# An attention and mixture-of-experts kernel on one core: the values products of the last 64 keys in quarters of the array, for both query groups at once

## The chip, the cores and the metric

The kernel runs on one core of a Trainium2 chip. TensorE does the matrix products (in the profile PE, its weight loads PEld), VectorE (DVE), ScalarE (ACT) and GpSimd (POOL) the work on rows, and SyncE (SP) issues every DMA. All data is fp32. The metric is the device time of one execution in microseconds; the changed kernel is compared with the kernel before on the same chip.

## The reference

Eight batches, eight heads, 576 positions, head size 64. First an attention with a bias from a small network on relative positions, then a soft mixture of experts over its output (512 wide, 32 slots, eight experts):

```python
scores = scale * np.matmul(q, k.transpose(0, 1, 3, 2))
...
bias = h @ w2
scores = scores + bias.transpose(2, 0, 1)[None, :, :, :]
scores = scores - np.max(scores, axis=-1, keepdims=True)
attn = np.exp(scores)
attn = attn / (np.sum(attn, axis=-1, keepdims=True) + 1e-09)
return np.matmul(attn, v).astype(np.float32)
```

The experts' part is `logits = x @ phi`, a softmax over all 4,608 tokens (dispatch) and one over the 32 slots (combine), `slot_input = d.T @ x`, two dense layers with a ReLU for each expert, and `c @ slot_out`.

## The kernel before, in words

A **unit** is one pair of heads of one batch: 4 pairs times 8 batches are 32 units, numbered pair by pair, so that units 24 to 31 are the last pair, where each batch's experts part is added. A unit's 576 queries are taken as row blocks p = 0 to 3 of 128 queries; the last 64 queries of two neighbouring units share a row block p = 4. The steps of a row block, named as in the order table:

- `S{p}.{n}`: the scores, half n of the keys, both heads at once: each product uses 64 rows of the array (line 438; line 443 for block 4, where four products use a quarter of the array each). Each head's result takes one of the eight PSUM banks.
- `t{p}.{head}{n}` (line 458, VectorE) adds the bias and finds the extreme, `e` (line 467, ScalarE) the exponential, `m` the reciprocal of the sums, `n` (line 373, GpSimd) the scaling.
- `T{p}` and `R{p}` (line 422) turn the weights so that keys lie on partitions: T the first 512 keys, R the last 64 of both heads, head 0 on partitions 0 to 63 and head 1 on 64 to 127. `c{p}` and `cR{p}` (line 376, ScalarE or VectorE) copy them to the tiles at0 (query group 0, blocks 0 and 1, 256 queries) and at1 (query group 1, the other 320 of each unit).

`M0` and `M1` (line 544) are the values products of the two query groups. Each is one accumulation in one bank over five blocks of keys, two heads each, every product on 128 rows and 64 columns of the array. For blocks 0 to 3 the 128 rows are 128 keys of one head. Block 4 holds the last 64 keys of *both* heads; its values come from the host in a form with zeros in the other head's 64 rows (`_apart`), so that half of the rows multiply zeros:

```python
for i in range(5):
    for hh in range(2):
        v0 = 64 * (4 * hh + i) if i < 4 else 512 + 64 * hh
        nc.tensor.matmul(po.t[64 * hh:64 * hh + 64, 0:w], d["v"][:, v0:v0 + 64],
                         main[:, :, 4 * hh + i, :] if i < 4 else x[:, r0:r0 + w], ...)
```

`x0` and `x1` copy the two results to a tile xts, and `xs` writes it to memory (line 557). `lq` and `lv` load a unit's queries and keys (line 342) and its values (line 347); `b0` to `b4` load the next pair's bias tiles bm and br (line 354), into five buffers for bm and one for br. `w` steps load expert weights (tile wt, lines 849 to 857), `fx` a batch's finished attention (tile xo, line 568). The experts' steps are `K`, `L` (line 611), `D` (lines 622 to 627), `W`, `Z` (lines 741 to 753), `C` and their copies; after the last one follow the two layers and the output (lines 961 to 1046).

Nothing here is scheduled at run time. The table `ORDER` lists every step as `name/unit`, in one sequence, with a + where a copy goes to VectorE instead of ScalarE; the steps are recorded in that order, so that it sets the order of the instructions on each engine and on SP's one queue. A PSUM bank is chosen at the step that first writes it, the one free the longest.

## Time and profile before

| | |
|---|---|
| time, median of 3 runs | 588.68 us (587.24 to 593.66) |
| the profiled execution | 590.42 us, span of the trace 588.6 us |
| TensorE busy | 557.2 us, 95% of the span |
| VectorE / ScalarE busy | 458.9 / 456.5 us, 78% each |
| GpSimd busy | 215.4 us, 37% |
| DMA | 111.90 MB, queue q1 53.9% of sixteen engines' time |

A busy TensorE is not yet a TensorE at its peak: an instruction counts as busy from its start to its modelled end, which overlaps its successor. What a group of products costs is read from the start of one group to the start of the next, or from the chain of waits, which lists them without overlap. An fp32 product shows as two records, so "x20" is ten products.

### The profile page before, as it was taken

The numbers are of one execution on the slowest core, as the hardware profiler recorded it, in microseconds if no ns is written. First come the engines' busy times: TensorE is split into PE (matmuls) and PEld (weight loads), VectorE is DVE, ScalarE is ACT, GpSimd is POOL, SyncE is SP. The second block draws the span as 40 slices with busy tenths as digits, with TensorE's granted clock in tenths as the row PEclk, the third lists the DMA queues.
The fourth block names the chain that finished last, engine by engine and source line by source line (L and its number), as shares of the span: only waits on it lengthen the run. The fifth ranks groups of instructions, "written<-read, shape, count | busy, mean of one in ns | idle before, by whom it ended". The sixth has DMA issues, their size and how long they took to land.

```text
span 588.6 us, 18890 instructions
## 1 busy us (share of the span) xinstructions
PE 557.2 (95%) x7175; PEld 356.9 (61%) x7175; DVE 458.9 (78%) x1807; ACT 456.5 (78%) x960; POOL 215.4 (37%) x311
## 2 busy tenths in 40 slices
PE   5899999999999999999999999799999999999993
PEld 3355666767666666666666666467666666653551
DVE  8999687888798887978898889487988988652323
ACT  6999789979978898887888798578767887841233
POOL 2001444554445446444445445244335223400000
PEclk9999899999999999999999999999999999999998
DMA  5599424044927364585515434821433406499988
GB/s 187 218 334 325 128 87 129 26 134 114 301 92 271 112 214 163 199 290 215 200 51 194 148 104 158 285 69 67 146 108 127 159 21 216 139 386 402 409 359 321
DMA packets 43322, 111.90 MB, mean 190 GB/s; under 512 B 7904, under 2 KB 8032, under 8 KB 43232
## 3 DMA queue, kind: packets, MB, share of 16 engines
q1 hardware_dynamic: 43232, 110.71, 53.9%
q8 instruction: 56, 0.92, 0.6%
q14 instruction: 34, 0.28, 0.1%
HBM read 83.28 MB, written 27.41 MB: 188 GB/s over the span
## 4 chain that ended last, share of the span: by engine, by line
PE 62%; DVE 12%; ACT 8%; DMA 7%; issue 5%; SPq 2%; POOL 2%; DVEq 0%; POOLq 0%; ACTq 0%
PE ps L544 17%; PE ps L438 15%; PE ps L422 12%; DVE y L458 6%; ACT y L467 3%; PE ps L443 3%; PE ps L1005 2%; PE ps L961 2%; DMA bm<-bias_m 2%; DMA xs<-xts 2%; PE ps L886 2%; POOL y L373 2%; SPq L354 2%; ACT e L896 2%; PE ps L611 2%
## 5 line engine op out<-in xcount | busy, mean ns | idle before, releaser
L373 POOL TENSOR_SCALAR y<-y,sm 128x576 f32<-128x576 f32 x288 | 210.5, 745 | 287.8 <-DVE sm L475 172.3
L467 ACT ACTIVATE y<-y,mn 128x576 f32<-128x576 f32 x288 | 221.1, 770 | 38.9 <-DVE mn L458 31.9
L544 PE MATMUL ps<-at,v 128*64 128x256 f32 (+1 forms) x1280 | 165.6, 409 | 1.3 <-DMA v<-in_v_dram 0.7
L376 ACT COPY at<-ps 128x1024 f32<-128x1024 f32 (+2 forms) x171 | 137.2, 817 | 27.7 <-PE ps L422 22.1
L438 PE MATMUL ps<-qk 64*128 64x288 f32 x1024 | 156.3, 422 | 1.9 <-DVE mn L458 1.7
L544 PEld LDWEIGHTS ps<-at,v 128*64 128x64 f32 x1280 | 88.5, 137 | 67.4 <-DVE mn L458 7.9
L458 DVE CUSTOM_DVE_ANT_0 y<-ps,bm,mn 128x288 f32<-128x288 f32 x256 | 123.1, 511 | 6.4 <-PE ps L438 2.9
L422 PEld LDWEIGHTS ps<-ident,y 64*128 64x128 f32 x2592 | 98.8, 140 | 43.3 <-issue 18.8
L458 DVE CUSTOM_DVE_ANT_0 y<-ps,bm 128x288 f32<-128x288 f32 x256 | 107.8, 453 | 21.6 <-PE ps L438 13.6
L422 PE MATMUL ps<-ident,y 64*128 64x64 f32 x2592 | 110.8, 228 | 6.7 <-POOL y L373 4.6
L438 PEld LDWEIGHTS ps<-qk 64*128 64x128 f32 x1024 | 95.2, 189 | 23.5 <-DVE mn L458 5.0
L467 ACT ACTIVATION_READ_ACCUMULATOR y<-y,mn 128x1 f32 x288 | 54.6, 190 | 0.0
L474 DVE TENSOR_SCALAR sm<-sm 128x2 f32<-128x2 f32 x144 | 38.0, 264 | 20.9 <-ACT y L467 20.4
L458 DVE DVE_READ_ACCUMULATOR2_ANT mn<- 128x1 f32 x576 | 47.5, 83 | 0.0
L886 PE MATMUL ps<-f,wbd 128*32 128x512 f32 (+49 forms) x640 | 42.0, 400 | 5.6 <-DVE f L877 3.3
L877 DVE TENSOR_SCALAR f<-tabs,scl,nb 128x560 f32<-128x560 f32 (+17 forms) x107 | 45.2, 496 | 1.4 <-PE ps L886 0.8
L376 DVE COPY at<-ps 128x256 f32<-128x256 f32 (+2 forms) x53 | 39.4, 743 | 8.3 <-PE ps L422 6.5
L886 PEld LDWEIGHTS ps<-f,wbd 128*32 128x32 f32 x640 | 20.8, 112 | 26.8 <-issue 9.3
L475 DVE RECIPROCAL sm<-sm 128x2 f32<-128x2 f32 x144 | 23.8, 166 | 4.9
L875 ACT ACTIVATE f<-tabs,cols,scl 128x416 f32<-128x416 f32 (+17 forms) x37 | 27.0, 791 | 0.0
L896 ACT ACTIVATE e<-ps,bcon 128x591 f32<-128x591 f32 x35 | 25.1, 784 | 0.0
L443 PE MATMUL ps<-qk 64*64 64x288 f32 x256 | 23.4, 435 | 0.0
(147 smaller groups left out, 361.6 us busy)
## 6 DMA issues: line engine op xcount, KB each, us to landing
wt<-in_moe_w_dram SPq DMA_DIRECT2D x62, 512.0 KB, 8.5
qk<-in_qk_dram SPq DMA_DIRECT2D x32, 608.0 KB, 4.1
v<-in_v_dram SPq DMA_DIRECT2D x32, 320.0 KB, 4.5
bias_m<-e SPq DMA_DIRECT2D x32, 295.5 KB, 3.6
out_dram<-ob SPq DMA_DIRECT2D x16, 512.0 KB, 5.2
xs<-xts SPq DMA_DIRECT2D x24, 288.0 KB, 4.5
xo<-xs SPq DMA_DIRECT2D x8, 864.0 KB, 5.0
bm<-bias_m SPq DMA_DIRECT2D x16, 288.0 KB, 3.9
```

Source lines behind the costliest of these rows:

```text
L373: nc.gpsimd.tensor_scalar(out=out, in0=y, scalar1=r, scalar2=1.0, op0=ALU.mult, op1=ALU.mult)
L376: (nc.vector.tensor_copy if eng else nc.scalar.copy)(out=out, in_=in_)
L422: nc.tensor.matmul(out, src[rs], ident[rs, rs], is_transpose=True, start=True, stop=True, tile_position=(64 * r, 0))
L438: nc.tensor.matmul(pss[hh].t[:, 0:HALF], x[rs, 640 + p * P:640 + (p + 1) * P], x[rs, k0:k0 + HALF], start=True, stop=True, tile_position=( ...
L443: nc.tensor.matmul(pss[hh].t[64 * r:64 * r + 64, 0:HALF], x[rs, 1152:1216], x[rs, k0:k0 + HALF], start=True, stop=True, tile_position=(64 ...
L458: nc.vector.tensor_tensor_reduce(out=d["y", p][:, hs], in0=d["ps", p, n][hh].read()[:, 0:HALF], in1=biases[hp][p][:, hs], scale=-QS, scala ...
L467: nc.scalar.activation(out=y, in_=y, func=AF.Exp, bias=d["mn", p][:, 2 + hh:3 + hh], scale=-1.0, accum_out=d["sm", p][:, hh:hh + 1])
L474: nc.vector.tensor_scalar(out=r, in0=r, scalar1=1e-9, scalar2=None, op0=ALU.add)
L544: nc.tensor.matmul(po.t[64 * hh:64 * hh + 64, 0:w], d["v"][:, v0:v0 + 64], main[:, :, 4 * hh + i, :] if i < 4 else x[:, r0:r0 + w], start= ...
L877: nc.vector.tensor_scalar(out=f, in0=tabs[:, 0:n], scalar1=sc, scalar2=nb1[:, 0:1], op0=ALU.mult, op1=ALU.max)
L886: nc.tensor.matmul(pb.t[32 * t:32 * t + 32, a // 512, a % 512:a % 512 + c1 - c0], wbd, x, start=True, stop=True, tile_position=(0, 32 * t))
L896: nc.scalar.activation(out=e, in_=x, func=AF.Identity, bias=bcon[:, k:k + 1])
```

## The change

Block 4 leaves `M0` and `M1`, which keep eight products each, and becomes a step `Mr`: four products that each use 64 rows and 64 columns of the array, one for each head and query group. For that query group 1 has its heads in exchanged halves of PSUM (and so of xts): head 0 of group 0 and head 1 of group 1 lie in partitions 0 to 63. Both groups' banks stay open from `M0` and `M1` until `Mr`. The values come without zeros (576 columns instead of 640), the keys of head 1 are rolled by 64 on the host instead of being stored twice (1,152 columns instead of 1,216). What R gives for group 0 goes to a tile of its own (`ar`, two buffers) instead of at0. Because of the exchange the experts' steps read some parts in other order, `phis` is kept a second time with its halves exchanged, and `rsum` shrinks to 32 columns, with its products split by columns. `ORDER` is a new table, with the step `Mr/u` added.

```diff
--- before.py
+++ after.py
@@ ORDER, two lines of some 176 @@
...
-S0.0/23 S0.1/23 e4.1/22 t2.11/22 t2.01/22 T1/22 m3/22 e4.0/22 e2.0/22 e2.1/22 n3.1/22 M1/21 n3.0/22 t0.10/23 t0.00/23
...
+T4/22 R4/22 t2.11/23 cR4/22 M0/22 K01/24 c4/22+ S3.1/23 t2.01/23 M1/22 t3.10/23 e1.1/23 t3.00/23 Mr/22 e0.0/23 m0/23
...
@@ -261,8 +262,8 @@
 
     ident = const.tile([P, P], F32, name="ident")
     make_identity(nc, ident)
-    rsum = const.tile([P, P], F32, name="rsum")
-    phis = const.tile([P, NP, NSL], F32, name="phis")
+    rsum = const.tile([P, 32], F32, name="rsum")
+    phis = const.tile([P, 2, NP, NSL], F32, name="phis")
     lp = xp.tile([P, 5 * P], F32, name="lp", tag="lp")
     et = xp.tile([P, 5 * P], F32, name="et", tag="et")
     et2 = xp.tile([P, 256], F32, name="et2", tag="et2")
@@ -294,13 +295,13 @@
 
     def ready():
 
-        nc.sync.dma_start(out=phis, in_=phi.rearrange("(g p) s -> p g s", p=P))
+        nc.sync.dma_start(out=phis[:, 0], in_=phi.rearrange("(g p) s -> p g s", p=P))
+        for r in range(2):
+            nc.sync.dma_start(out=phis[64 * r:64 * r + 64, 1], in_=phi.rearrange("(g r p) s -> p r g s", r=2, p=64)[:, 1 - r])
         nc.gpsimd.tensor_scalar(out=phis, in0=phis, scalar1=-1.0, scalar2=None, op0=ALU.mult)
-        nc.gpsimd.tensor_add(out=rsum[:, 0:32], in0=ident[:, 0:32], in1=ident[:, 32:64])
-        nc.gpsimd.tensor_add(out=rsum[:, 0:32], in0=rsum[:, 0:32], in1=ident[:, 64:96])
-        nc.gpsimd.tensor_add(out=rsum[:, 0:32], in0=rsum[:, 0:32], in1=ident[:, 96:128])
-        for r in range(1, 4):
-            nc.gpsimd.tensor_copy(out=rsum[:, 32 * r:32 * r + 32], in_=rsum[:, 0:32])
+        nc.gpsimd.tensor_add(out=rsum, in0=ident[:, 0:32], in1=ident[:, 32:64])
+        nc.gpsimd.tensor_add(out=rsum, in0=rsum, in1=ident[:, 64:96])
+        nc.gpsimd.tensor_add(out=rsum, in0=rsum, in1=ident[:, 96:128])
         for t in (lp, et, et2):
             nc.gpsimd.memset(t, 0.0)
 
@@ -338,12 +339,12 @@
 
 
         hp, b = units[u]
-        x = st[u]["qk"] = ldp.tile([P, 1216], F32, name="qk", tag="qk")
+        x = st[u]["qk"] = ldp.tile([P, 1152], F32, name="qk", tag="qk")
         nc.sync.dma_start(out=x, in_=qk[b, hp])
 
     def load_v(u):
         hp, b = units[u]
-        x = st[u]["v"] = ldp.tile([P, 640], F32, name="v", tag="v")
+        x = st[u]["v"] = ldp.tile([P, 576], F32, name="v", tag="v")
         nc.sync.dma_start(out=x, in_=v[b, hp])
 
     biases = [{} for _ in range(NP)]
@@ -432,15 +433,15 @@
             pss = d["ps", p, n] = [Banks(1), Banks(1)]
             for hh in range(2):
                 rs = slice(64 * hh, 64 * hh + 64)
-                k0 = 64 * (1 - hh) + n * HALF
+                k0 = n * HALF
                 if p < 4:
                     x = d["qk"]
-                    nc.tensor.matmul(pss[hh].t[:, 0:HALF], x[rs, 640 + p * P:640 + (p + 1) * P], x[rs, k0:k0 + HALF],
+                    nc.tensor.matmul(pss[hh].t[:, 0:HALF], x[rs, S + p * P:S + (p + 1) * P], x[rs, k0:k0 + HALF],
                                      start=True, stop=True, tile_position=(64 * hh, 0))
                 else:
                     for r in range(2):
                         x = st[u + r]["qk"]
-                        nc.tensor.matmul(pss[hh].t[64 * r:64 * r + 64, 0:HALF], x[rs, 1152:1216], x[rs, k0:k0 + HALF],
+                        nc.tensor.matmul(pss[hh].t[64 * r:64 * r + 64, 0:HALF], x[rs, S + 512:2 * S], x[rs, k0:k0 + HALF],
                                          start=True, stop=True, tile_position=(64 * hh, 64 * r))
 
         for n in range(2):
@@ -497,7 +498,7 @@
 
             o = st[u - u % 2] if c else d
             if ("at", c) not in o:
-                o["at", c] = atp.tile([P, (9, 54)[c] * (256, 64)[c]], F32, name="at", tag=f"at{c}")
+                o["at", c] = atp.tile([P, (8, 54)[c] * (256, 64)[c]], F32, name="at", tag=f"at{c}")
             return o["at", c]
 
         if p < 4:
@@ -516,8 +517,9 @@
                         half_turn(pt.t[:, r, 64 * i:64 * i + 64], d["y", q][:, 512:640], r)
 
             def keep_rest(eng):
-                o0 = (2048, 3136)[c]
-                o = target()[:, o0:o0 + 256].rearrange("a (i r n) -> a r i n", i=2, r=2)
+                if c == 0:
+                    d["ar"] = atp.tile([P, 256], F32, name="ar", tag="ar", bufs=2)
+                o = (target()[:, 3136:3392] if c else d["ar"]).rearrange("a (i r n) -> a r i n", i=2, r=2)
                 if p == 4:
                     o = target()[:, 3072:3456].rearrange("a (b i n) -> a b i n", i=1, n=64)[:, 0:6:5]
                 k = len(qs)
@@ -526,34 +528,47 @@
             step(u, f"R{p}", turn_rest)
             step(u, f"cR{p}", keep_rest)
 
-    def mix(u, c):
+    def mix(u):
 
         d = st[u]
         hp, b = units[u]
-        w = 256 + 64 * c
-
-        def products(_):
+        wide = (256, 320)
+
+        def source(c):
+            return (st[u - u % 2] if c else d)["at", c]
+
+        def products(c):
             po = d["po", c] = Banks(1)
-            x = (st[u - u % 2] if c else d)["at", c]
             b0 = u % 2 if c else 0
-            main = x[:, 0:(4, 6)[c] * 512].rearrange("a (b k n) -> a b k n", k=8, n=64)[:, b0:b0 + 4 + c]
-            r0 = (2048, 3072 + 64 * b0)[c]
-            for i in range(5):
+            main = source(c)[:, 0:(4, 6)[c] * 512].rearrange("a (b k n) -> a b k n", k=8, n=64)[:, b0:b0 + 4 + c]
+            for i in range(4):
                 for hh in range(2):
-                    v0 = 64 * (4 * hh + i) if i < 4 else 512 + 64 * hh
-                    nc.tensor.matmul(po.t[64 * hh:64 * hh + 64, 0:w], d["v"][:, v0:v0 + 64],
-                                     main[:, :, 4 * hh + i, :] if i < 4 else x[:, r0:r0 + w], start=i == 0, stop=i == 4,
-                                     tile_position=(0, 64 * hh))
-
-        step(u, f"M{c}", products)
-
-        def keep(eng):
+                    o = 64 * (hh ^ c)
+                    nc.tensor.matmul(po.t[o:o + 64, 0:wide[c]], d["v"][:, 64 * (4 * hh + i):64 * (4 * hh + i) + 64],
+                                     main[:, :, 4 * hh + i, :], start=i == 0, stop=False, tile_position=(0, o))
+
+        def rest(_):
+            r0 = 3072 + 64 * (u % 2)
+            keys = d["ar"], source(1)[:, r0:r0 + 320]
+            for hh in range(2):
+                rs = slice(64 * hh, 64 * hh + 64)
+                for c in range(2):
+                    o = 64 * (hh ^ c)
+                    nc.tensor.matmul(d["po", c].t[o:o + 64, 0:wide[c]], d["v"][rs, 512:576],
+                                     keys[c][rs], start=False, stop=True, tile_position=(64 * hh, o))
+
+        for c in range(2):
+            step(u, f"M{c}", lambda _, c=c: products(c))
+        step(u, "Mr", rest)
+
+        def keep(eng, c):
             if "xt" not in d:
                 d["xt"] = xp.tile([P, S], F32, name="xts", tag="xt", bufs=2)
-            cp(eng, d["xt"][:, 256 * c:256 * c + w], d["po", c].read()[:, 0:w])
-
-        step(u, f"x{c}", keep)
-        if c == 1 and hp < NP - 1:
+            cp(eng, d["xt"][:, 256 * c:256 * c + wide[c]], d["po", c].read()[:, 0:wide[c]])
+
+        for c in range(2):
+            step(u, f"x{c}", lambda eng, c=c: keep(eng, c))
+        if hp < NP - 1:
             step(u, "xs", lambda _: nc.sync.dma_start(out=xs[b, hp], in_=d["xt"]))
 
     def moe(u):
@@ -606,25 +621,29 @@
 
         def logits(_):
             pl = m["L"] = Banks(2)
-            for n in range(2):
+            for n, (a0, j0, j1) in enumerate(((256, 0, 256), (0, 256, S))):
                 for g in range(NP):
-                    nc.tensor.matmul(pl.t[32 * g:32 * g + 32, n, 0:HALF], phis[:, g, :],
-                                     X(g)[:, n * HALF:(n + 1) * HALF], start=True, stop=True, tile_position=(0, 32 * g))
+                    nc.tensor.matmul(pl.t[32 * g:32 * g + 32, n, a0:a0 + j1 - j0], phis[:, n, g, :], X(g)[:, j0:j1], start=True,
+                                     stop=True, tile_position=(0, 32 * g))
 
         step(u, "L", logits)
-        step(u, "lc", lambda eng: cp(eng, lp[:, 0:S].rearrange("a (x n) -> a x n", x=2), m["L"].read()[:, :, 0:HALF]))
+        step(u, "lc", lambda eng: cp(eng, lp[:, 0:S], m["L"].read().rearrange("a x n -> a (x n)")[:, 256:256 + S]))
         parts = ((0, slice(0, P)), (1, slice(P, 192)))
 
         def dispatch(_):
             pr = m["D"] = Banks(1 + fin, 3)
             if fin:
                 for n in range(2):
-                    nc.tensor.matmul(pr.t[:, n, 0:HALF], rsum, lp[:, n * HALF:(n + 1) * HALF], start=True, stop=True)
+                    for g in range(4):
+                        nc.tensor.matmul(pr.t[32 * g:32 * g + 32, n, 0:HALF], rsum, lp[:, n * HALF:(n + 1) * HALF], start=True,
+                                         stop=True, tile_position=(0, 32 * g))
                 return
             for cc in range(4):
-                nc.tensor.matmul(pr.t[32 * cc:32 * cc + 32, 0:P], rsum[:, 0:32], lp[:, cc * P:(cc + 1) * P], start=True,
+                nc.tensor.matmul(pr.t[32 * cc:32 * cc + 32, 0:P], rsum, lp[:, cc * P:(cc + 1) * P], start=True,
                                  stop=True, tile_position=(0, 32 * cc))
-            nc.tensor.matmul(pr.t[:, P:192], rsum, lp[:, 512:576], start=True, stop=True)
+            for g in range(4):
+                nc.tensor.matmul(pr.t[32 * g:32 * g + 32, P:192], rsum, lp[:, 512:576], start=True, stop=True,
+                                 tile_position=(0, 32 * g))
 
         step(u, "D", dispatch)
 
...
@@ -913,8 +938,7 @@
     for u, (hp, b) in enumerate(units):
         for p in range(5 - u % 2):
             rows(u, p)
-        for c in range(2):
-            mix(u, c)
+        mix(u)
         if hp == NP - 1:
             moe(u)
         if u >= 2:
@@ -932,7 +956,7 @@
     homes.update(wbr=(bsp, "br"), wat0=(atp, "at0"), wat1=(atp, "at1"), wv=(ldp, "v"), wxo=(xp, "xo"), wxt=(xp, "xt"),
                  wxk=(xp, "xk"))
     for k, home in homes.items():
-        step(U - 1, k + {"wv": " M1", "wxt": " K23 KR L x1"}.get(k, ""), lambda _, home=home: fetch_w(home, several.get(home[1], 1)))
+        step(U - 1, k + {"wv": " Mr", "wxt": " K23 KR L x1"}.get(k, ""), lambda _, home=home: fetch_w(home, several.get(home[1], 1)))
 
     csts, ends, hT2 = {}, {}, {}
 
...
-
 def _lay(q, k, v):
 
     B, H, S, D = q.shape
     q, k, v = (x.reshape(B, H // 2, 2, S, D) for x in (q, k, v))
     qt, kt = q.swapaxes(3, 4), k.swapaxes(3, 4)
-    kt = np.concatenate([kt[..., 512:], kt], axis=-1)
-    qk = np.concatenate([kt.reshape(B, H // 2, 128, 640), qt.reshape(B, H // 2, 128, 576)], axis=-1)
+    kt = np.stack([kt[:, :, 0], np.roll(kt[:, :, 1], 64, axis=-1)], axis=2)
+    qk = np.concatenate([kt, qt], axis=-1).reshape(B, H // 2, 128, 1152)
     vm = v[:, :, :, 0:512].reshape(B, H // 2, 2, 4, 128, D).transpose(0, 1, 4, 2, 3, 5).reshape(B, H // 2, 128, 512)
-    return qk, np.concatenate([vm, _apart(v[:, :, :, 512:])], axis=-1)
+    return qk, np.concatenate([vm, v[:, :, :, 512:].reshape(B, H // 2, 128, D)], axis=-1)
 
 
 def kernel(**inputs):
```

The table's lines tell nothing by themselves, so the order of the instructions is shown at three places. First TensorE around the values products of unit 12, before:

```order
L544 MATMUL ps<-at,v 64x320 x10
L544 MATMUL ps<-at,v 64x256 x10
L422 MATMUL ps<-ident,y 128x64 x20
L438 MATMUL ps<-qk 128x288 x4
L422 MATMUL ps<-ident,y 128x64 x16
```

and now:

```order
L547 MATMUL ps<-at,v 64x256 x8
L423 MATMUL ps<-ident,y 128x64 x18
L439 MATMUL ps<-qk 128x288 x4
L547 MATMUL ps<-at,v 64x320 x8
L557 MATMUL ps<-ar,v 64x256
L557 MATMUL ps<-at,v 64x320
L557 MATMUL ps<-ar,v 64x256
L557 MATMUL ps<-at,v 64x320
L423 MATMUL ps<-ident,y 128x64 x36
```

Twenty products in 128 rows and 64 columns have become sixteen and four quarters; here M0 comes ahead of M1, with transposes and scores between, so that M0's bank is held through them.

Second, TensorE around the scores of row block 4 of units 12 and 13 (line 443 before, 444 now), before:

```order
L438 MATMUL ps<-qk 128x288 x2
L544 MATMUL ps<-at,v 64x256 x10
L443 MATMUL ps<-qk 64x288 x8
L422 MATMUL ps<-ident,y 128x64 x20
L438 MATMUL ps<-qk 128x288 x8
```

and now:

```order
L423 MATMUL ps<-ident,y 128x64 x20
L444 MATMUL ps<-qk 64x288 x4
L557 MATMUL ps<-ar,v 64x256
L557 MATMUL ps<-at,v 64x320
L557 MATMUL ps<-ar,v 64x256
L557 MATMUL ps<-at,v 64x320
L444 MATMUL ps<-qk 64x288 x4
L423 MATMUL ps<-ident,y 128x64 x16
```

Here the quarter products of unit 11 stand between two groups of scores that divide the array in the same way.

Third, SP's queue where the last pair's bias tiles are loaded (units 22 to 24), before:

```order
L354 DMA br<-bias_r 64x512
L354 DMA bm<-bias_m 128x576
L354 DMA bm<-bias_m 128x64
L354 DMA bm<-bias_m 128x512
L557 DMA xs<-xts 128x576
L849 DMA wt<-in_moe_w_dram 128x1024
L568 DMA xo<-xs 128x3x576
L347 DMA v<-in_v_dram 128x640
L849 DMA wt<-in_moe_w_dram 128x1024
```

and now:

```order
L355 DMA bm<-bias_m 128x576
L355 DMA bm<-bias_m 128x64
L355 DMA bm<-bias_m 128x512
L348 DMA v<-in_v_dram 128x576
L572 DMA xs<-xts 128x576
L343 DMA qk<-in_qk_dram 128x1152
L348 DMA v<-in_v_dram 128x576
```

Each fence ends a few rows behind the last bias tile. Before, the results xs, a weight tile, the 864 KB of xo, values and another weight tile follow it; now xo stands ahead of br, no weights follow, and behind the last tile come a load of values, an xs and a load of queries and keys. The last three bm tiles now stand directly behind each other.

## Rows read from the trace of the kernel before

**Rows 1.** The page, part 1: busy time, share of the span, instructions.

```profile
PE 557.2 (95%) x7175; PEld 356.9 (61%) x7175; DVE 458.9 (78%) x1807; ACT 456.5 (78%) x960; POOL 215.4 (37%) x311
```

**Rows 2.** Windows by stage: length, busy time (instructions) by engine, clock, DMA share, GB/s.

```profile
16.00:60.00 44.00, 41.58 (x604) 21.07 (x596) 41.74 (x120) 42.88 (x72) 3.05 (x5) 1.00 0.81 290
...
440.00:480.00 40.00, 39.64 (x554) 25.22 (x550) 35.91 (x143) 32.21 (x76) 13.42 (x20) 1.00 0.33 112
480.00:520.00 40.00, 39.94 (x562) 25.45 (x562) 29.20 (x115) 30.84 (x75) 13.39 (x21) 1.00 0.52 177
520.00:588.60 68.60, 56.51 (x737) 29.33 (x729) 23.86 (x54) 20.94 (x42) 0.00 (x0) 0.96 0.95 376
```

**Rows 3.** Windows of two pairs of units in the middle, engines as above.

```profile
227.80:253.85 26.05, 25.83 (x324) 17.25 (x323) 22.48 (x96) 22.63 (x49) 13.18 (x18) 1.00 0.64 213
```

**Rows 4.** Chain of waits, 214.8 to 294.5 us: start, length, what, records.

```profile
273.30 2.84 PE ps L544 x20
...
281.37 5.00 PE ps L544 x40
...
292.18 2.31 PE ps L544 x20
```

**Rows 5.** TensorE's timeline: start, length, records, idle time before in brackets.

```profile
267.87 1.20 PE L443 MATMUL ps<-qk 64*64 64x288 f32 x16
269.00 0.34 PE L422 MATMUL ps<-ident,y 64*128 64x64 f32 x4
```

**Rows 6.** The same at 437 us, a single group of four.

```profile
437.05 0.72 PE L443 MATMUL ps<-qk 64*64 64x288 f32 x8
437.70 0.52 PE L422 MATMUL ps<-ident,y 64*128 64x64 f32 x9
```

**Rows 7.** The same at 294 us.

```profile
294.42 1.66 PE L443 MATMUL ps<-qk 64*64 64x288 f32 x16
296.02 0.65 PE L422 MATMUL ps<-ident,y 64*128 64x64 f32 x12
```

**Rows 8.** Groups of TensorE instructions by form: count, busy us, mean ns, idle before.

```profile
L443 PE MATMUL ps<-qk 64*64 64x288 f32 x256 | 23.4, 435 | 0.0
```

**Rows 9.** VectorE's timeline at 372 us.

```profile
372.50 0.08 DVE L458 DVE_READ_ACCUMULATOR2_ANT mn<- 128x1 f32 x1
377.04 0.46 DVE L458 CUSTOM_DVE_ANT_0 y<-ps,bm 128x288 f32<-128x288 f32 x1 [4.46 <-DMA bm<-bias_m]
```

**Rows 10.** SP's timeline there: when each DMA was issued.

```profile
369.59 1.48 SPq L354 DMA_DIRECT2D bm<-bias_m  x3
371.16 0.38 SPq L557 DMA_DIRECT2D xs<-xts  x1
371.58 0.43 SPq L849 DMA_DIRECT2D wt<-in_moe_w_dram  x1
372.06 0.43 SPq L568 DMA_DIRECT2D xo<-xs  x1
```

**Rows 11.** TensorE's timeline there.

```profile
378.04 0.71 PE L422 MATMUL ps<-ident,y 64*128 64x64 f32 x16 [1.02 <-DVE mn L458]
381.06 0.46 PE L422 MATMUL ps<-ident,y 64*128 64x64 f32 x8 [2.31 <-POOL y L373]
381.78 0.68 PE L422 MATMUL ps<-ident,y 64*128 64x64 f32 x12 [0.26 <-POOL y L373]
```

**Rows 12.** Windows of the stall and of what follows it.

```profile
376.00:382.00 6.00, 2.40 (x40) 1.56 (x38) 3.06 (x15) 3.20 (x8) 1.74 (x3) 1.00 0.96 344
382.00:386.00 4.00, 4.00 (x48) 2.48 (x46) 2.66 (x11) 1.60 (x3) 2.63 (x4) 0.57 0.56 164
```

**Rows 13.** The page, part 6: DMA issues, KB each, us to landing.

```profile
wt<-in_moe_w_dram SPq DMA_DIRECT2D x62, 512.0 KB, 8.5
...
bm<-bias_m SPq DMA_DIRECT2D x16, 288.0 KB, 3.9
```

**Rows 14.** TensorE's timeline at 567 us, four products in four strips of rows.

```profile
567.10 0.66 PE L1046 MATMUL ps<-sst,cR 32*64 32x256 f32 x8
567.69 1.07 PE L1005 MATMUL ps<-wt,hT 128*32 128x256 f32 x16
```

**Rows 15.** Timeline at 54 us: GpSimd's first use on y.

```profile
54.24 1.47 POOL L373 TENSOR_SCALAR y<-y,sm 128x576 f32<-128x576 f32 x2 [42.73 <-ACT e L896]
```

369 lines of the change are left out of this document (185 added, 184 removed).

## The prediction

> **What bounds the kernel now.** I read the busy shares first: TensorE 95%, VectorE and ScalarE 78% each [rows 1]. A mean hides stages, so the windows come next [rows 2]. From 16 to 60 us, where the bias tables are made, VectorE and ScalarE are full (41.74 and 42.88 of 44.00 us). In the middle, two neighbouring units take 26.05 us, of which TensorE is busy 25.83, VectorE 22.48 and ScalarE 22.63 [rows 3]. From 440 to 520 us TensorE is full again. In the tail from 520 us the DMA engines are busy 95% of the time. So between about 65 and 520 us a piece of TensorE's work that goes is worth its length, as long as nothing else fills the gap, and the other two engines have about 14% to spare.
>
> **What the removed products cost.** The chain of waits has the values products without overlap [rows 4]: ten of 320 columns 2.84 us, ten of 256 columns 2.31 us, and both behind each other 5.00 us. Apart they cost 0.15 us more than together, and the difference is one more change in how the array is divided. So one change costs 0.15 us, and five blocks of keys for both groups 5.00 - 0.15 = 4.85 us. One block of a unit is 0.97 us: 0.54 with 320 columns ((2.84 - 0.15)/5) and 0.43 with 256.
>
> **What the added products cost.** Products in quarters are in the trace: the scores of row block 4, 288 columns. Two groups of four take 1.13 us from their start to the next instruction [rows 5], one group 0.65 [rows 6]: one group more is 0.48, and 0.17 is the change of division. 288 columns in 0.48 us is the rate of 320 columns in 0.54, so four quarters run at once, and Mr takes 0.54 us, the longer of its two widths. Gain: 32 units x (0.97 - 0.54) = **13.8 us**. Against it stand the changes of division. Counted along TensorE's order, the array is divided in 232 stretches before and 249 now, because Mr stands alone in some places and beside products of its own kind in others: 17 x 0.15 = **2.6 us**. Net 11.2 us, the upper end.
>
> The trace shows no Mr, so the lower end needs a bound. Groups of four are not always that quick: two took 1.60 us at 294 us [rows 7], 0.47 more than the clean ones, and all 32 groups took 23.4 us [rows 8], 0.73 each, where a clean one with half a change is 0.57. If Mr pays the whole excess of 0.16 to 0.17, that is 32 x 0.165 = 5.3 us, and the gain is 5.9. Those scores are slow where a bank has not been read yet; Mr's banks are already held, but it must wait for two copies of the last keys. It is like them in part, so I take half of the excess, 2.6: a gain of **8.6 us**, with ends 5.9 and 11.2.
>
> **What the new order does to the stall at 377 us.** VectorE sat idle 4.46 us there for a bias tile of the last pair [rows 9]. It was issued at 369.59 us, and right behind it the queue got xs, 512 KB of weights and 864 KB of xo [rows 10]; it landed some 6 us later, where 3.9 is usual [rows 13]. TensorE stood still 1.02 + 2.31 + 0.26 us [rows 11]. After that idle time its granted clock fell: 0.57 in the mean from 382 to 386 us [rows 12], the lower level of 1.2 GHz for most of these 4 us, which loses another 0.43 x 4 = 1.7 us. The stall costs 5.3 us. In the new order neither weights nor xo follow these tiles, and between the issue of the second-last tile and its first use stand four adds of another block, some 2 us, and products. A landing in 3.9 us would still be waited for about 1 us. I take **4.3 us** as the gain, between 0 (the stall only moves to another tile) and 5.3.
>
> **The rest.** The three new small loads and the wider phis lie ahead of GpSimd's first use on y, before which it idles 42.73 us [rows 15]; without that cover they would be a few us once. Queries, keys and values shrink by 2.1 MB of 111.90 MB, which no wait in the middle asks for. The dispatch product over the last tokens is split by columns: its two changes of division go and are in the count of 17. Copies stay the same in number; some change between VectorE and ScalarE, and both have room [rows 3]. Four weight loads of 512 KB move from before unit 24 to after it; from 440 to 520 us the DMA share is 0.33 and 0.52 [rows 2], which hides them. Were the tail to wait for them, 2.1 MB at its 376 GB/s would be 5.6 us.
>
> **Sum.** The profiled execution took 590.42 us, of which the span is 588.6, and lies 1.7 above the median of the runs. 590.4 - 8.6 - 4.3 = 577.5; put on the median, 588.7 - 12.9 = **575.8 us**. Its own ends are 588.7 - 5.9 = 582.8 (slow Mr, stall moved) and 588.7 - 11.2 - 5.3 = 572.2.
>
> **Rivals.**
>
> *The new order saves more.* If it also sheds the excess of the scores in quarters, 5.3 us, by putting Mr and these scores beside each other: 588.7 - 11.2 - 5.3 - 5.3 = 567 us. For it speaks that about half of the 32 Mr stand so; against it, that these scores are slow for want of a read bank, which their place does not change.
>
> *The gain comes back as waits for banks.* M0's and M1's banks are held until Mr, with scores between that need two banks each. A score that finds its bank unread cost 0.47 us more [rows 5, 7]. One such wait in each unit is 15.0 us: 588.7 - 11.2 - 4.3 + 15.0 = 588.2, no change. For it speaks that VectorE, which reads the banks of the scores, is busy 86% of a pair of units [rows 3]; against it, that in about a quarter of the units M0, M1 and Mr stand directly behind each other.
>
> *The same wait twice a unit, and the kernel is slower.* Between M0 and Mr, TensorE's queue is in order: behind one waiting score stand the turns that feed the copies for Mr, and Mr behind those holds both banks longer. Two waits of 0.47 in each unit are 30.1 us: 588.7 - 15.5 + 30.1 = 603 us. It decides from (15.5 + 5.9)/32 = 0.67 us of new waiting in each unit. Against it: in the pair of units shown TensorE is idle only 0.22 us, so there is no sign of starved banks now.
>
> *The quarters do not run at once.* Mr's two halves of rows write the same two banks, in different partitions; the scores in quarters use a bank for each half of rows. The nearest row is the product of four strips of 32 rows in the output stage, where strips 0 and 1 write two halves of one bank: 0.59 us from its start to the next instruction [rows 14]. One strip behind the other in each bank would be at least 2 x 0.43 + 0.15 = 1.01. So the trace speaks against it. If Mr did run in two rounds, it would cost 1.08 us in place of 0.54: 32 x (0.97 - 1.08) = -3.5, less 2.6, so 588.7 + 6.1 - 4.3 = 590.5. The Trainium skill, "TensorEngine Tiling (Array Packing)", section "Restrictions and Gotchas", states this rival as a rule: different row tiles cannot access the same PSUM bank at the same time. By that rule Mr takes two rounds; the trace's row does not agree for disjoint partitions.
>
> **How the numbers follow.** A measurement of this kernel tells about 1% from no change. Forecast 56%, more saved 14%, gain eaten 15%, two rounds 5%, slower 10%. Predicted is the forecast's time, 576. The range takes in the saving order at its own low end (567 less 3 us, if still more waits go) and, above, the eaten gain, 588.2 with a little over: 564 to 589. Outside stay the two cases above it, 15%, and a few per cent below. Faster by over 1% means under 582.8: the forecast but for its upper edge (54%) and the saving order, 68%. Within 1%: that edge, the eaten gain and the two rounds, 22%. Slower by over 1%: 10%.
>
> **What the profile after would show.** Mr's four products take 0.54 us and a change of division, about 0.7 us from start to next start; 1.2 would mean two rounds. The values products of blocks 0 to 3 take 0.43 and 0.54 us a block as before. A pair of units in the middle takes 25.2 to 25.6 us instead of 26.05. VectorE's wait for bm near unit 24 is under 1.5 us, and TensorE's clock does not fall there. I am wrong if TensorE's waits on VectorE before scores or on copies before Mr pass 0.5 us a unit, or if the tail waits for weights.

## The result, and the profile after

The changed kernel took 583.78 us in the median of 13 runs (580.87 to 586.29), the kernel before 590.27 in as many on the same chip: 0.9891 of its time, 95% interval 0.9867 to 0.9915. It is faster by 1.1%; predicted were 2.2%. Two more sets of runs, each beside the kernel before on the same chip, gave 0.9876 [0.9836, 0.9916] and 0.9889 [0.9857, 0.9921]. Two of the 99 runs of the kernel before fell in a slower state of the chip and are left out of its means.

The page's first part answers to [rows 1]: TensorE works 10.9 us less, VectorE 6.3 less, ScalarE 3.5 more.

```profile
PE 546.3 (94%) x7235; PEld 351.7 (61%) x7235; DVE 452.6 (78%) x1808; ACT 460.0 (79%) x959; POOL 217.6 (38%) x308
```

Mr is line 557 now, the other values products 547, the scores in quarters 444. By form (count, busy us, mean ns, idle before), answering to [rows 8]:

```profile
L557 PE MATMUL ps<-at,v 64*64 64x320 f32 x128 | 23.9, 448 | 0.0
L444 PE MATMUL ps<-qk 64*64 64x288 f32 x256 | 22.6, 429 | 1.5 <-ACT at L377 1.2
L557 PE MATMUL ps<-ar,v 64*64 64x256 f32 x128 | 20.8, 395 | 0.0
```

One Mr in TensorE's timeline (start, length, records), with what stands ahead and behind:

```profile
243.96 0.34 PE L423 MATMUL ps<-ident,y 64*128 64x64 f32 x4 [0.20 <-POOL y L374]
244.23 0.43 PE L557 MATMUL ps<-ar,v 64*64 64x256 f32 x1
244.23 0.48 PE L557 MATMUL ps<-at,v 64*64 64x320 f32 x1
244.24 0.43 PE L557 MATMUL ps<-ar,v 64*64 64x256 f32 x1
244.25 0.48 PE L557 MATMUL ps<-at,v 64*64 64x320 f32 x1
...
244.55 0.44 PE L557 MATMUL ps<-at,v 64*64 64x320 f32 x2
244.71 1.26 PE L444 MATMUL ps<-qk 64*64 64x288 f32 x16
```

From its start to the next group's, which divides the array in the same way, are 0.48 us. All four products begin within 0.02 us, though two and two write halves of one bank, and together they take as long as one: the quarters run at once. Over all 32 units Mr takes 0.43 to 0.83 us from its start to the next instruction: 0.43 in the median where both neighbours have its own division, 0.70 where neither has.

Windows of pairs of units, as [rows 3], and the place of the old stall, as [rows 12]:

```profile
231.15:257.20 26.05, 25.64 (x325) 17.55 (x322) 22.10 (x96) 23.02 (x49) 12.54 (x18) 1.00 0.74 238
257.20:283.10 25.90, 24.89 (x314) 17.40 (x312) 20.11 (x91) 23.27 (x50) 12.87 (x18) 1.00 0.71 241
```

```profile
379.00:383.00 4.00, 4.00 (x62) 1.00 0.35 136
383.00:387.00 4.00, 4.00 (x35) 1.00 0.42 145
```

A pair takes hardly less than before, though TensorE has less to do in it. The stall is gone: full clock, TensorE never idle. In the whole trace VectorE's waits for tiles bm are down from one of 4.46 us [rows 9] to the row below (us in total, times, longest), and none of them lies near unit 24:

```profile
DVE y L459 <- DMA bm<-bias_m: 1.5, 2, 0.9
```

New are short waits of TensorE on the passage into the tail (timeline; idle time before in brackets), where the kernel before had two over 0.2 us, of 0.64 and 0.93:

```profile
509.22 0.42 PE L626 MATMUL ps<-xo,phis 128*32 128x256 f32 x3 [0.89 <-DMA xo<-xs]
...
514.30 0.49 PE L717 MATMUL ps<-ident,lp 32*128 32x32 f32 x5 [0.69 <-ACT lp L377]
...
517.01 1.43 PE L776 MATMUL ps<-xk,ek 128*32 128x128 f32 x40 [0.57 <-ACT ck L750]
518.92 0.33 PE L971 MATMUL ps<-ident,accs 128*128 128x128 f32 x1 [0.47 <-DVE accs L782]
519.60 1.92 PE L986 MATMUL ps<-wt,sT 128*32 128x512 f32 x16 [0.35 <-ACT sT L973]
```

The last row is the first product with experts' weights: the tail starts at 519.60 us, in the kernel before at 530.46. Up to there the trace shows a gain of 10.9 us (two more traces of the changed kernel, 10.0 and 8.8); end to end the runs show 6.5. So the question is what happens at and behind this place.

### The profile page after: what moved, and what is told of

Read it like the earlier page. It is cut to its first block, busy times and chain, and to the rows that moved or that the text cites. A ratio compares the mean times of both kernels' runs of the same rounds, so it can differ in the third digit from the quotient of the medians.

```text
span 579.5 us, 19040 instructions
## 1 busy us (share of the span) xinstructions
PE 546.3 (94%) x7235; PEld 351.7 (61%) x7235; DVE 452.6 (78%) x1808; ACT 460.0 (79%) x959; POOL 217.6 (38%) x308
## 4 chain that ended last, share of the span: by engine, by line
PE 64%; DVE 11%; ACT 10%; DMA 6%; issue 4%; POOL 2%; SPq 0%; ACTq 0%; POOLq 0%; DVEq 0%
PE ps L547 16%; PE ps L439 16%; PE ps L423 13%; DVE y L459 6%; ACT y L468 4%; PE ps L444 3%; PE ps L557 3%; PE ps L1030 2%; POOL y L374 2%; PE ps L986 2%; ACT f L900 2%; PE ps L911 2%; ACT e L921 2%; DMA bias_m<-e 1%; DMA xo<-xs 1%
## 5 line engine op out<-in xcount | busy, mean ns | idle before, releaser
L439 PE MATMUL ps<-qk 64*128 64x288 f32 x1024 | 160.2, 422 | 1.2 <-DMA qk<-in_qk_dram 0.4
L377 ACT COPY at<-ps 128x1024 f32<-128x1024 f32 (+2 forms) x151 | 132.1, 895 | 23.2 <-PE ps L423 19.3
L547 PE MATMUL ps<-at,v 128*64 128x320 f32 (+1 forms) x1024 | 133.7, 410 | 0.7 <-DMA v<-in_v_dram 0.4
L423 PE MATMUL ps<-ident,y 64*128 64x64 f32 x2592 | 113.3, 227 | 3.4 <-DVE mn L459 1.0
L439 PEld LDWEIGHTS ps<-qk 64*128 64x128 f32 x1024 | 100.3, 187 | 18.7 <-DVE mn L459 2.8
L547 PEld LDWEIGHTS ps<-at,v 128*64 128x64 f32 x1024 | 70.4, 137 | 54.6 <-DVE mn L459 6.9
L911 PE MATMUL ps<-f,wbd 128*32 128x79 f32 (+45 forms) x640 | 43.4, 407 | 7.0 <-DVE f L902 4.2
L911 PEld LDWEIGHTS ps<-f,wbd 128*32 128x32 f32 x640 | 22.8, 114 | 27.9 <-issue 10.1
L377 DVE COPY at<-ps 128x1024 f32<-128x1024 f32 (+2 forms) x41 | 31.2, 763 | 5.5 <-PE ps L423 5.0
L900 ACT ACTIVATE f<-tabs,cols,scl 128x432 f32<-128x432 f32 (+15 forms) x38 | 26.5, 753 | 2.5 <-DMA bias_m<-e 2.5
```

Source lines behind the costliest of these rows:

```text
L377: (nc.vector.tensor_copy if eng else nc.scalar.copy)(out=out, in_=in_)
L423: nc.tensor.matmul(out, src[rs], ident[rs, rs], is_transpose=True, start=True, stop=True, tile_position=(64 * r, 0))
L439: nc.tensor.matmul(pss[hh].t[:, 0:HALF], x[rs, S + p * P:S + (p + 1) * P], x[rs, k0:k0 + HALF], start=True, stop=True, tile_position=(64 * ...
L547: nc.tensor.matmul(po.t[o:o + 64, 0:wide[c]], d["v"][:, 64 * (4 * hh + i):64 * (4 * hh + i) + 64], main[:, :, 4 * hh + i, :], start=i == 0 ...
L900: nc.scalar.activation(out=f, in_=tabs[:, 0:n], func=AF.Relu, bias=cols[:, 1:2], scale=sc)
L911: nc.tensor.matmul(pb.t[32 * t:32 * t + 32, a // 512, a % 512:a % 512 + c1 - c0], wbd, x, start=True, stop=True, tile_position=(0, 32 * t))
```

## The experiments

All are edits of the changed kernel unless it says otherwise. The table has all runs of a kernel together, over several chips (the kernel before's from all sets of runs but the first); "lost" is one minus the mean granted clock, times the run's time. The kernel before's means differ by some 1.5 us from chip to chip, so where a difference is small it is also given against the kernel before on the same chip.

| kernel | runs | median us | mean us | clock | lost us |
|---|---|---|---|---|---|
| before | 84 | 589.66 | 589.86 | 0.9908 | 5.4 |
| changed | 25 | 583.46 | 583.55 | 0.9865 | 7.9 |
| last block in whole rows | 12 | 593.59 | 593.62 | 0.9861 | 8.3 |
| scaling halved | 5 | 578.21 | 578.63 | 0.9878 | 7.1 |
| scaling halved, whole rows | 12 | 589.84 | 590.00 | 0.9883 | 6.9 |
| waits filled | 18 | 581.48 | 581.41 | 0.9899 | 5.9 |
| before, waits filled | 12 | 591.02 | 590.56 | 0.9906 | 5.6 |

**The changed kernel again.**

> The changed kernel unchanged, for the others of this call to stand against. Every theory: 583 us or so (it took 583.78 in the median, 6.5 us under the kernel before), with its single runs spread from 581 to 586 us. Its trace shows whether a typical run loses its 2 us over the 581.3 us of the profiled one in one place (a stretch of lower granted clock, a late tile) or evenly; evenly if the granted clock alone does it.

582.74 us. Its trace has the clock low behind the first of the short waits (windows: length, TensorE busy, clock, DMA share, GB/s):

```profile
505.00:509.00 4.00, 3.15 (x28) 0.96 1.04 402
509.00:513.00 4.00, 4.00 (x48) 0.61 1.02 396
```

That is mostly the lower level of 1.2 GHz, behind a wait of 0.85 us. In the profiled execution both windows have 1.00, behind a wait of 0.89. A third trace of the changed kernel has the longest such wait, 1.75 us, and the clock stays full in it too. So it happens in some runs and not in others, not evenly, and the length of this one wait doesn't decide it.

**The products alone.**

```diff
-nc.tensor.matmul(po[c][o:o+64], v[rs, 512:576], keys[c][rs], tile_position=(64*hh, o))
+nc.tensor.matmul(po[c][o:o+64], v[:, 512:576], keys[c], tile_position=(0, o))
```

> The changed kernel's order and loads, but the last block of each unit again as two column pairs over whole rows (four products of 128 rows in two rounds instead of four quarters in one; the values are not separated by head there, so this part of the output is not the reference's). Theory A, the quarters save what they should on TensorE (0.43 us a unit) and the gain is lost elsewhere: 32 x 0.43 = 13.8 us slower than the changed kernel in the same call, 597 us, that is some 7 us slower than the kernel before, because the new order's 17 more changes of the array's division and its waits stay. Theory B, VectorE or ScalarE sets the pace in the steady middle and TensorE's saving is swallowed there: only 4 to 8 us slower than the changed kernel, 588 to 592 us. Theory C, the four quarters run in two rounds: no slower, 583 to 585 us.

593.59 us: 10.1 slower than the changed kernel by the means of all runs, 10.6 beside it on one chip. That lies between theories A and B; C is out. Against the kernel before it is 1.0052 [1.0025, 1.0079]: the same products in the new order, 3.2 us slower by the means on that chip, 3.8 against all runs. Its Mr:

```profile
248.55 0.65 PE L556 MATMUL ps<-ar,v 128*64 128x256 f32 x4
249.03 0.71 PE L556 MATMUL ps<-at,v 128*64 128x320 f32 x4
249.67 1.20 PE L444 MATMUL ps<-qk 64*64 64x288 f32 x16
```

1.12 us instead of 0.48, 0.15 of it a change of division. Added up over the 32 units, from start to next start, Mr takes 35.1 us here and 20.8 in the changed kernel: TensorE saves 14.2 us. This pair of runs splits the result: quarters -10.1, order +3.8 (on one chip -10.6 and +3.2). So some 4 us of what the quarters save on TensorE do not reach the end.

**Quarters in the old order.** Kernel before; in the 15 units where M1 and M0 already stand together, block 4 becomes quarters directly behind them.

```diff
-for i in range(5):            # blocks 0 to 4, each group
+for i in range(4 if u in QUARTERS else 5):
...
+# behind the second of M0, M1: four quarters for both groups
```

> The kernel before with its order and loads, and quarters only in the 15 units whose M0 and M1 already stand one directly behind the other (units 2 to 18 by twos, 23 to 29 by twos, 30 and 31). The exchange of the second group's heads is left out, so its part of the output is not the reference's. Its divisions change 245 times, 13 more than before. Theory A, TensorE's time is what counts and the new order gave gain back in waits: 15 x 0.43 less 13 x 0.15 = 4.5 us faster than the kernel before, 585.5 us, or 0.30 us a unit. Theory B, the copies and VectorE bound the middle: under 2 us faster, 588 to 590 us. If it gains more a unit than the changed kernel does (6.5 / 32 = 0.20 us), the new order costs something that this one does not.

597.93 us, 1.013 [1.0083, 1.0176] of the kernel before: neither theory. By the first scores of each unit its trace gained 0.6 us from unit 8 to unit 20; it lost 3.2 from unit 26 to unit 31 and 5.3 more up to the tail. In units 23, 25, 27, 29, 30 and 31 each xts is now complete only after both groups, and TensorE waits on the passage into the tail. That the one makes the other is my reading (timeline, windows):

```profile
512.19 1.96 PE L752 MATMUL ps<-xk,ek 128*32 128x256 f32 x16 [2.07 <-DVE ek L377]
```

```profile
508.00:512.00 4.00, 2.12 (x30) 0.99 0.00 1
512.00:516.00 4.00, 3.81 (x40) 0.58 0.00 0
534.00:538.00 4.00, 3.54 (x56) 0.73 0.93 331
538.00:542.00 4.00, 3.10 (x18) 0.50 1.01 346
```

Its tail starts at 539.34 us. The quarters hold both results to the end of the unit, and put into the old order they made the program slower.

**Weights earlier.** `w0/19` to `w0/23` moved to units 19 to 21.

> The changed kernel with the last five weight tiles (w0/19 to w0/23) loaded from unit 19 on, one a unit, instead of at units 27 to 29. Theory A, the 1.75 us that the end grew by, and the 0.9 us wait for an input of the tail, come from weight transfers that stand in the way of the tail's own loads and the outputs: 1 to 2.6 us faster than the changed kernel, 581 to 583 us. Theory B, the queue at the end is full with the outputs themselves: no change (within 0.5 us). Theory C, the weights now crowd the loads of units 19 to 23 and the stall at unit 24 is back: 2 to 5 us slower, 586 to 589 us.

582.79 us, no change: the weights are not it. In its trace the wait for the tail's input is 1.13 us and the outputs' last stretch 8.7 us, both as long as in the changed kernel's traces.

**Half of GpSimd's scaling.**

```diff
-nc.gpsimd.tensor_scalar(out=out, in0=y, scalar1=r, ...)
+nc.gpsimd.tensor_scalar(out=out[:, 0:288], in0=y[:, 0:288], scalar1=r, ...)
```

> The changed kernel, with GpSimd scaling only the first 288 of each score tile's 576 columns (the other half stays unscaled, so the output is not the reference's). This shortens one scaling from 0.75 us to about 0.4 us and brings each scaled tile some 0.35 us earlier to the transposes that wait for it; no other engine's work changes. In the steady middle a pair of units has two groups of 20 transposes that take 1.17 and 1.28 us instead of 0.65. Theory A, the softmax chain that ends at GpSimd keeps the rest of the quarters' gain in the middle: up to 0.35 us at two places a pair, some 15 pairs: 5 to 10 us faster than the changed kernel's 582.7 us, 573 to 578 us. Theory B, the throughput of VectorE or ScalarE (83% and 88% busy in the middle) keeps it: under 2 us faster, 581 to 583 us.

> The same half scaling together with the last block in whole rows (four products of 128 rows, two rounds, values not separated by head) instead of quarters; the output is not the reference's for both reasons. Against the run with half scaling and quarters this prices the quarters with the chain out of the way. Theory A (the chain swallowed what TensorE saved): the difference is larger than the 10.9 us measured with full scaling, 13 to 15 us (32 x 0.43 = 13.8 and four changes of division more, 0.6): 587 to 592 us, the same as or faster than the kernel before. Theory B (VectorE and ScalarE): the difference stays near 10.9 us, 592 to 594 us.

578.21 and 589.84 us: 4.9 and 3.6 faster by the means than with full scaling (one scaling took 0.51 us, not 0.4). The quarters are worth 11.4 us here against 10.1 to 10.6, nearer to theory B; the difference is no larger than its noise (standard error 0.8). So the full scaling keeps at most a small part of the quarters' gain. How much of the 4.9 and 3.6 is the chain through GpSimd is not shown: in both traces the last stretch behind the last copy, where GpSimd does nothing, is 7.75 us, against 9.3 and 9.0 with full scaling.

**The tail's input first.** `wy1 wbm2 wy2 fx/31` becomes `fx/31 wy1 wbm2 wy2`.

> The changed kernel, with the last input tile of the tail's first part (fx/31) issued ahead of the three weight loads that now stand directly before it on SyncE. Theory A, the changed kernel loses time at the passage into the tail, where TensorE waits 0.85 to 0.9 us for that tile 8.1 us after its issue (before it landed 5.1 us after) and the granted clock fell to half for some 3.5 us behind the wait in one of two traces: the wait goes, 0.9 us, and where the clock fell another 1.7 us, so 0.9 to 2.6 us faster than the changed kernel's median of 582.7 us, 580 to 582 us, with mean granted clocks of 0.989 to 0.992 more often than 0.982 to 0.986. Theory B, the clock falls elsewhere too (the other waits of 0.35 to 0.7 us at 515 to 520 us): 0.5 to 1 us faster, the clocks as before. Theory C, the three weights now come late to the tail: no change or slower.

583.06 us, no change, so theory A is out and B's 0.5 us do not show either. The 0.9 us wait is gone, but in this trace the clock fell at the next waits instead (0.70, 0.59, 0.47, 0.35 us at 512 to 519 us):

```profile
509.00:513.00 4.00, 3.30 (x65) 1.00 1.03 410
513.00:517.00 4.00, 3.41 (x73) 0.72 1.02 393
517.00:521.00 4.00, 3.17 (x24) 0.50 1.05 405
```

This fall has a price that can be read. From the tail's first product to the end of the last copy the changed kernel takes 50.6 us, and so does every trace in which the clock is full from the tail's start on; here, with the low clock reaching some 2.7 us into the tail, it takes 52.0.

**The stall alone, in the kernel before.** `fx/24` ahead of `lq/24`, `w0/21` and `w0/22` to units 18 and 19.

> The kernel before, products and order of TensorE untouched; only its loads are moved so that the bias tile that VectorE waits 4.46 us for near 375 us comes earlier: the input tile fx/24 is issued ahead of lq/24, and the weights w0/21 and w0/22 three and five units earlier. Theory A, as the prediction had it: the stall's 3.6 us of idle TensorE and the fall of the clock behind it, 5.3 us in all, are saved, 585 us. Theory B, most of what is saved there comes back as waits further on, as it seems to have done in the changed kernel: 588 to 590 us. Theory C, another load is late in its place: no change, 590 us or more.

590.88 us, 1.0017 [0.9993, 1.0042]. The edit took only part of the stall (timeline of VectorE; windows of TensorE):

```profile
377.05 0.46 DVE L458 CUSTOM_DVE_ANT_0 y<-ps,bm 128x288 f32<-128x288 f32 x1 [2.50 <-DMA bm<-bias_m]
```

```profile
376.00:382.00 6.00, 4.29 (x58) 1.00 0.41 149
382.00:386.00 4.00, 4.00 (x48) 0.57 0.55 149
```

The clock still fell. From unit 22's first scores to unit 26's this trace takes 57.7 us, the kernel before 59.6; so 1.9 us were saved there, and the runs are no faster. New waits came elsewhere, one of 1.7 us for an xs on VectorE and one of 1.0 on TensorE behind it. With part of the stall left it does not test the stall's whole price.

**The old opening.** The first 378 steps in the kernel before's order, the rest in the new one.

> The changed kernel with the opening in the order of the kernel before: all steps up to the first scores of unit 2 stand as they stood there (with unit 0's quarters put behind its M1), everything behind them as in the changed kernel. Theory A, the new order gives back in the opening what it saves later: the scores of unit 2 began at 79.0 us in the changed kernel and at 77.4 us before, although one unit's quarters (0.4 us) were already saved there, and unit 2 of the run with whole rows began at 79.9 us. Then this kernel is 1.6 to 2.5 us faster than the changed one's 583.4 us (median of 31 runs of it and of two versions that took the same time), 581 to 582 us. Theory B, the opening's loss is made up further on by waits that are there anyway: no change, within 0.7 us.

593.45 us: it tests neither theory. The seam has stalls of its own; the scores of unit 2 began at 86.9 us instead of 79.0. The opening's 1.6 us stay a reading of single traces, which scatter: unit 2 begins at 77.4 to 78.5 us in four traces with the old order's opening and at 78.5 to 80.4 in eight with the new one's. Together with filled waits:

> The old opening and the filled waits together. If each is worth what its theory A says, 1.6 to 2.5 us and about 2 us, they add: 579 to 580 us, 1.8% under the kernel before. If the opening's gain is swallowed, 581 to 582 us; if neither holds, 583 us.

593.18 us, the same seam.

**Filled waits.** Transposes of the identity into the bank that the waiting product writes next, 3, 2, 2, 1 and 1 of them:

```diff
+def fill(bank, n):
+    for _ in range(n):
+        nc.tensor.transpose(out=bank[:, 0:P], in_=ident, identity=ident)
```

> The changed kernel with nine transposes of the identity (0.27 to 0.33 us each) put into five waits of TensorE on the passage into the tail (0.85, 0.70, 0.59, 0.47 and 0.35 us in the traces), each group less than its wait, so that it is busy in them; their results are overwritten. Theory A, the changed kernel's typical runs lose about 2 us to a granted clock that falls to half behind these waits (the traces show it at 508 to 513 us in one run and at 514 to 521 us in another; its runs lost 7.8 us of full clock in the mean, those of the kernel before 5.7): the falls are gone, the mean granted clock is 0.990 or more, 581 to 582 us. Theory B, the clock falls there for another reason, or elsewhere: no change, 583 to 584 us, clocks of 0.982 to 0.989 as before. Theory C, the fillers themselves come late: 0.3 to 1 us slower.

> The changed kernel with nine transposes of the identity in five waits on the passage into the tail, once more. Its first six runs had granted clocks of 0.990 or more in five, but stood to the kernel before on that chip as the changed kernel did on others (0.9891). Theory A, the falls of the clock there cost about 2 us: beside the changed kernel on the same chip it is 1 to 2 us faster, with a mean clock of 0.989 or more. Theory B, the time they cost is lost anyway (the tail's transfers or the outputs set the end): the clock is higher, the time the same within 0.5 us. Theory C, the six clocks were chance: clock and time as the changed kernel's.

> The filled version of the changed kernel a third time, beside it: 0.985 to 0.989 of the kernel before, 581.5 us in the middle, clock 0.990. Its trace shows a third time whether the stretch from the last copy to the end is 7.5 us, as in its first two traces, or 8.4 to 9.3, as in the three of the changed kernel.

581.82, 580.79 and 581.15 us; 0.9891 [0.9850, 0.9932], 0.9849 [0.9816, 0.9882] and 0.9856 [0.9825, 0.9887] of the kernel before. The changed kernel beside the second took 583.22 us. All runs together: 2.1 us faster than the changed kernel (standard error 0.4); with each measured against the kernel before on its own chip, 1.4 us (standard error 0.7). A mean clock under 0.988 came in 15 of 25 runs of the changed kernel and in 1 of 18 of this one. The first six runs left it open (the clock up, the ratio as before); the three sets together speak for theory A, with a gain of 1.4 to 2.1 us.

**The same in the kernel before**, five transposes in its two waits:

> The kernel before, with five transposes of the identity in its own two longer waits on the passage into the tail (0.64 and 0.93 us in its trace). Theory A, the falls of the clock there belong to the changed kernel's passage with its five waits: the kernel before gains nothing from it, within 0.7 us of 590 us, its mean granted clock stays at about 0.990. Theory B, the falls are as frequent in both: 1 to 2 us faster, 588 to 589 us, and the 2 us that the filled version of the changed kernel gained say nothing of this change.

591.01 us, 1.0014 [0.9989, 1.0038]; clock 0.9906, without them 0.9908. By this interval there is no more than 0.7 us to gain there: the loss on the passage belongs to the changed kernel.

**The opening filled too**, eight more transposes at 60 to 65 us:

> Also eight transposes in three waits of unit 0 (1.04, 0.95 and 0.73 us, at 60 to 65 us in the traces), behind which the granted clock was at half for 3.4 to 6.9 us in every trace of the changed kernel. Theory A, the clock is worth its time there: another 1 to 2.5 us faster, 579 to 581 us. Theory B, VectorE and ScalarE set the pace in that stretch (TensorE waits for them in it), so the half clock costs nothing there: no change against the other filled version. Theory C, the fillers delay what they stand ahead of: up to 1 us slower.

581.97 us; theory B. The windows of the version with the tail alone filled, and of this one:

```profile
60.00:64.00 4.00, 1.76 (x26) 0.80 0.66 208
64.00:68.00 4.00, 4.00 (x50) 0.50 0.28 76
68.00:72.00 4.00, 4.00 (x40) 0.85 0.46 147
```

```profile
60.00:64.00 4.00, 2.93 (x32) 1.00 0.70 205
64.00:68.00 4.00, 2.95 (x51) 1.00 0.40 111
68.00:72.00 4.00, 3.21 (x36) 1.00 0.47 147
```

The clock is full and the time is the same: TensorE does the same work sooner and then waits 1.39 us for VectorE, which sets the pace there. In these runs a low clock cost time on the passage, where TensorE sets the pace, and none here.

## Why the prediction was half right

**The products: right.** Mr was to take 0.54 us and about 0.7 with a change; it took 0.43 to 0.48 in the median where the group behind has its own division, and 0.70 between others. Two rounds are refuted. The Trainium skill, "TensorEngine Tiling (Array Packing)", section "Restrictions and Gotchas", states that different row tiles cannot access the same PSUM bank at once; the trace does not agree where they write different partitions of it.

**The gain of 8.6 us: near, in part by luck.** For the quarters alone, in one order, the terms give -13.8 - 4 x 0.15 + 2.6 = -11.8; measured were -10.1 to -10.6, and -11.4 with the scaling halved. The 2.6 stood for a slow Mr, and Mr is not slow: TensorE saves 14.2 us on it, where the terms without the 2.6 say 14.4. What keeps some 4 us of that from the end lies elsewhere; one place is the steady middle, where units 8 to 19 gain 3.0 to 4.2 us against whole rows in place of their share of 5.3.

**The sign in the middle: wrong.** 25.2 to 25.6 us a pair were promised, 26.05 and 25.90 came. I had spread the 17 new changes of division evenly, but counted along the trace's records 14 of them (56 against 42) lie in the 12 steady units 8 to 19. From unit 8's first scores to unit 20's these took 158.0 us before, 159.4 with whole rows in the new order, 156.3 now.

**A gain at the tail's start carried to the end in full: this step failed.** The terms for the order alone are 21 x 0.15 = 3.2 for its changes with whole rows and -4.3 for the stall, -1.1; measured were +3.2 on one chip, +3.8 over all runs. The term for the stall did not fail. Unit 22's first scores, unit 26's and the tail's first product, in the trace before and in that of the new order with whole rows:

```profile
339.71 1.19 PE L438 MATMUL ps<-qk 64*128 64x288 f32 x8
399.29 0.76 PE L438 MATMUL ps<-qk 64*128 64x288 f32 x4
530.46 1.92 PE L961 MATMUL ps<-wt,sT 128*32 128x512 f32 x16 [0.93 <-ACT sT L949]
```

```profile
344.48 1.19 PE L439 MATMUL ps<-qk 64*128 64x288 f32 x8
397.77 1.19 PE L439 MATMUL ps<-qk 64*128 64x288 f32 x8
529.91 1.50 PE L985 MATMUL ps<-wt,sT 128*32 128x512 f32 x12 [0.35 <-ACT sT L972]
```

The stall's stretch takes 53.3 us instead of 59.6, and the new order has no idle TensorE and no fall of the clock in it:

```profile
376.00:382.00 6.00, 6.00 (x57) 1.00 0.18 70
382.00:386.00 4.00, 3.97 (x62) 1.00 0.24 56
```

The 6.3 us are not the stall's price alone, since the two orders differ there in other steps too. Ahead of it the new order had lost 4.8 us, half of that in the opening (unit 2's scores at 79.9 us, before at 77.4). So up to the tail's start the sum is about right: 0.55 us earlier than before, where the terms say 1.1.

Behind it, it is not. The sum counts what is gained by the tail's start as gained at the end, and "The rest" asked there only whether the tail waits for weights, which it does not. Two things that I had priced at nothing come there.

One lies on the passage: with its waits filled, lost clock goes from 7.9 to 5.9 us and the time falls by 1.4 to 2.1, in the changed kernel only.

The other is the last stretch, from the last copy's end to the end of the span:

```profile
569.62 0.58 ACT L1074 COPY obr<-ps 128x512 f32<-128x512 f32 x1 [0.23 <-PE ps L1071]
```

570.20 to 579.5 are 9.3 us; two more traces of the changed kernel have 9.0 and 8.4, those with earlier weights and with the tail's input first 8.7 and 9.1, whole rows 9.0; the kernel before and three versions of it 7.6 to 7.9. The three traces with filled waits have 7.5, but the two with the scaling halved, which fill nothing, have 7.75. So what sets this stretch is open, and so is how the fillers' gain divides between clock and outputs.

Of the order's miss of 4.3 to 4.9 us, the last stretch makes 1.4 in the pair of traces. They end only 0.9 us apart, the runs 3.2 to 3.8: the profiled execution of whole rows was a quick one (591.32 us, the mean 593.62). No trace shows a typical one, and why the rest is lost is not settled. Lost clock, 8.3 us in the mean and 4.7 in that execution, is the one number on record that goes with it. That 583.8 us comes out near the prediction's own slow end of 582.8 is luck: that end stood for a slow Mr and a stall that only moves, and neither came.

**The rivals.** More saved: no. Gain eaten by waits for banks: not as priced; the single waits of TensorE on other engines that the trace names in the steady units are 0.3 us at most. Slower products can hide more, and some 4 us of the quarters' saving are missing. Slower through late results: not in the changed kernel. The old order with quarters is 7 us slower, with late results on the passage into the tail; the rival had put them, twice a unit, between M0 and Mr.

## What to carry to other kernels

Price a new order apart from the new instructions: the same products in the new order take one kernel, and it showed 3.2 to 3.8 us lost where the sum had 1.1 gained. A gain in one stage is worth its length only if the stages behind it take it over without new gaps: price the next passage and the last transfers too, and not only the loads that moved. Where TensorE sets the pace, several short waits close together may cost twice, as time and as clock; cheap products that depend on nothing, put into them, got 1.4 to 2.1 us back here, and where another engine sets the pace they got nothing.

## What the hardware showed unexpectedly

VectorE's small `TENSOR_SCALAR` on the sums is held by GpSimd. Timeline at 240 us:

```profile
240.58 1.47 POOL L374 TENSOR_SCALAR y<-y,sm 128x576 f32<-128x576 f32 x2 [4.86 <-DVE sm L476]
...
241.51 0.56 DVE L475 TENSOR_SCALAR sm<-sm 128x2 f32<-128x2 f32 x1 [0.25 <-ACT y L468]
```

It began 0.54 us before GpSimd's second scaling ended (242.05) and ended with it. Of the 59 that began during a scaling, 34 took over 0.3 us, and 32 of these ended within 0.08 us of its end; the 85 others took 0.17 at most. Of the 59, four ran through in 0.17 us with most of a scaling still ahead; they had begun within 0.12 us of its start. Count, minimum, median and maximum of the changed kernel, then with the scaling halved:

```profile
L475 DVE TENSOR_SCALAR sm<-sm x144: 147/168/749, 58.1 to 497.7; 128x2 f32<-128x2 f32 x144
```

```profile
L475 DVE TENSOR_SCALAR sm<-sm x144: 148/166/440, 57.8 to 495.0; 128x2 f32<-128x2 f32 x144
```

The longest falls from 749 to 440 ns with the shorter scaling. So part of what the halved scaling gains may be this. The Trainium skill, "SBUF — State Buffer", section "SBUF: two separate sides", describes a port pair that VectorE and GpSimd share and that one of them holds for a whole instruction; the trace agrees for this instruction, with the 32 that ended with the scaling.
